# Moving a routing step, the last token transfer and the last weight casts in an attention and top-1 expert kernel

## The chip, the cores and the metric

The kernel runs on one core of one Trainium2 chip. The metric is the device time of one execution in microseconds (us). Before the change three runs took 266.01, 266.17 and 263.75 us, with a median of 266.01. One more execution was profiled.

## The reference

Linear attention without softmax over 8 batches of 8 heads, 576 tokens and 64 columns a head; its output, normed and laid out as 4608 tokens of 512 columns, goes through a layer of 8 experts, of which each token uses the one with the highest gate logit.

```python
kv = np.einsum('bhsd,bhse->bhde', k, v)
out = np.einsum('bhsd,bhde->bhse', q, kv)
rms = np.sqrt(np.mean(out * out, axis=-1, keepdims=True) + 1e-06)
x = out / rms * g_norm                 # as (4608, 512)
logits = x @ w_gate
expert_idx = np.argmax(logits, axis=1)
# gate_w: softmax probability of the chosen expert
h = np.maximum(x[expert_idx == e] @ w1[e], 0.0)      # 512 -> 1024
out[expert_idx == e] = gate_w * (h @ w2[e])          # 1024 -> 512
```

All inputs are drawn at random in f32.

## The kernel before, in words

The order of the instructions on every engine is written by hand (`manual_schedule`): an engine runs its instructions in the order in which the program emits them, and a waiting instruction holds up those behind it. There are three stages.

**Attention, in slots.** Before the loop, 92 products of zeros (`zeros`, L876, 64 columns each) run on PE while the first k and v load. Then 36 slots of 128 tokens follow. In slot `s`, `x_mm(s)` (L343) multiplies 128 transposed q rows by the batch's kv matrix, which holds the gate's columns as well; `x_qt(s+2)` (L320) transposes a later q block; `x_norm(s)` squares the product (`sq`, ACT, L361) and sums it (`ms`, DVE, L365). From slot 31 on the rest of a slot, `held`, comes one slot late: logarithm and exponential on ACT (`lnt`, `rinv`), the scaled logits (`lr`, DVE, L373) and the scaled rows (`xh`, DVE, L381). What else a slot does is put on lists by `at(list, slot, function)`: `mid` runs straight after `x_mm`, `pre` after `sq` and `ms` are issued, `late` near the end of the slot.

**Routing, in groups of 2 to 5 slots.** For each group, class `Route` finds the expert of each token and the token's row within that expert's part of the scratch tensor `xs_scratch`: `logits`, `top`, `below` (`dl`), `code`, `first`, `choose`, `tally` (`cum`, L445) on DVE; `expo` (ACT, L469, `ex`, the exponentials for the gate); `ranks`, three products on PE (L461, L462, L465) that write into unused columns of the PSUM tile of a slot; then `mask` (L473), `send` (row numbers `sli`, L481, and gate sums, L483) and `total` (L453) on DVE; and `scatter`, one indirect DMA for each slot, issued by POOL (L491). The list `plan` gives each group's slots in the order sum, below, one-hot, rank, then the slots of its scatters. Group (3, 0, 4), the first four slots of the last pair of batches, is the one whose entry changes. The next group, (3, 4, 3), is the `rt` of the lines after `plan`; the last one is called `end`.

**Experts.** `jobs[e]` holds expert e's tokens: 608 for each of the first seven, 672 for the last, which is given an expert with many tokens. `fetch` reads them on SP's queue: the marks `mt` (L683, and L691 for the last 32 tokens of job 7) and a transposing DMA `xt` (L675). `one` multiplies by w1 (L731) and applies relu on ACT (L743); `two` multiplies by w2 (L797), 128 tokens a tile; `put` scales on DVE (`ys`, L805) and POOL scatters the rows to the output (L808). Job 7 has a sixth tile of 32 tokens, spread over 128 partitions (L789). For expert 0, the first 384 tokens are fetched when the routing of most slots is done (`jobs[0].fetch(0, NE)`, in slot 30), so that its first products (`early_one`, `early_pair`, tile `hpe`) run between the last routing steps. The rest of its tokens (tile `hpl`) waits for all scatters.

Weights arrive on SP's queue in f32 (`load1` at L165 and `load2` at L171, 2 MB each) and are cast to f16: w1 on DVE (L177) or ACT (L183), w2 on ACT (L188, `cast2`) or, where `cast2` is given an engine, on DVE (L190). SP's queue is one line: loads and fetches are issued and moved in the program's order. In the loop over experts, iteration n runs job n and issues, after its `one` products, the next load and then the fetch of job n+3. In iteration 4 that load is w2 of expert 7, and the fetch behind it is job 7's. During iteration n the weights of expert n+1 are cast: w1 in the first half of the `one` products, w2 between the tiles of `two`.

Of the kernel before, what the change touches and what calls it, by code (L numbers as in the profile page):

```python
# [21 lines left out]
def _bc(ap: bass.AP, insert_pos: int, count: int) -> bass.AP:  # L22
    dims = [list(d) for d in ap.ap]
    dims.insert(insert_pos, [0, count])
    return bass.AP(tensor=ap.tensor, offset=ap.offset, ap=dims)
# [3 lines left out]
def kernel(  # L29
# [11 lines left out]
    nc = tc.nc  # L41
# [4 lines left out]
    E = 8  # L46
    F = 1024
    RW = 516
    CT = 5
# [3 lines left out]
    NE = EARLY // 128  # L53
# [142 lines left out]
    def load_next(count=1):  # L196
        nonlocal n_loads
        for _ in range(count):
            if n_loads < len(loads):
                n, m = loads[n_loads]  # L200
                (W[n].load1 if m == 1 else W[n].load2)(stg[n_loads % 5], nc.sync)
                n_loads += 1
# [93 lines left out]
    def split(s):  # L296
        P, r = divmod(s, 9)
        b = 2 * P + (r >= 4)
        return P, r, b
# [34 lines left out]
    def x_mm(s):  # L334
        P, r, b = split(s)
        if r < 8:
            parts = [(slice(0, 128), kvs_bufs[b % 4])]
        else:
            parts = [(HALF[tok], kvs_bufs[(2 * P + tok) % 4]) for tok in range(2)]
        ops[s] = quad("kvp" if s in (32, 35) else "op", "op")  # L340
        for i4 in range(4):
            for cols, kvs in parts:
                nc.tensor.matmul(  # L343
                    ops[s][cols, i4, 0:144], qts[s][:, i4, cols], kvs[:, i4, :],
                    start=True, stop=True,
                )

    def x_norm(s):
        P, r, b = split(s)
        if r == 0:  # L350
            xgs[P] = xh[P % 2][:, 0:9 * RW].rearrange("p (g c) -> p g c", g=9)
            lrs[P] = PW.tile([128, 9, 8, 8], F32, tag="lr", bufs=2, name="lr")
        if r == (2, 2, 2, 3)[P]:
            nc.gpsimd.tensor_copy(
                xgs[P][:, :, 512:514].bitcast(I32).rearrange("p g o -> p (g o)"),
                tokc[:, 9 * P:9 * P + 9],
            )
        xg, lr = xgs[P], lrs[P]
        oc = ops[s]
        sq = PW.tile([128, 8, 64], F32, tag="sq", bufs=1, name="sq")  # L360
        nc.scalar.activation(  # L361
            sq.rearrange("p (c i) n -> p c (i n)", i=2), oc[:, :, 0:128], ACTF.Square
        )
        ms = PW.tile([128, 8], F32, tag="ms", bufs=3, name="ms")
        nc.vector.reduce_sum(ms, sq, axis=AXX)  # L365

        def scale():
            lnt = PW.tile([128, 8], F32, tag="lnt", bufs=3, name="lnt")
            nc.scalar.activation(lnt, ms, ACTF.Ln, scale=1.0 / 64.0, bias=epsb)
            rinv = PW.tile([128, 8], F32, tag="rinv", bufs=3, name="rinv")  # L370
            nc.scalar.activation(rinv, lnt, ACTF.Exp, scale=-0.5)  # L371
            r2 = rinv.rearrange("p (c i) -> p c i", i=2)
            nc.vector.tensor_tensor(  # L373
                lr[:, r, :, :].rearrange("p (c i) n -> p c i n", i=2),
                oc[:, :, 128:144].rearrange("p c (i n) -> p c i n", i=2),
                _bc(r2, 3, 8), op=ALU.mult,
            )
            return r2

        def rows(r2):  # L380
            nc.vector.tensor_tensor(  # L381
                xg[:, r, 0:512].rearrange("p (i c n) -> p c i n", i=2, c=4),
                oc[:, :, 0:128].rearrange("p c (i n) -> p c i n", i=2),
                _bc(r2, 3, 64), op=ALU.mult,
            )

        def rest():
            r2 = scale()
            return lambda: rows(r2)

        return rest
# [441 lines left out]
    def expert_at(t):  # L833
        return nc.values_load(
            tabi[0:1, 0, bass.ds(t, 1)], engines=[ENG.SP],
            min_val=0, max_val=E - 1,
        )
# [16 lines left out]
    jobs = []  # L854
# [10 lines left out]
    with tc.tile_pool(name="psattn", bufs=1, space=bass.MemoryType.PSUM) as PSA:  # L865
        first_slot = [9 * (b // 2) + 4 * (b % 2) for b in range(B)]
        mid, pre, head, late, last = ({s: [] for s in range(-4, 40)} for _ in range(5))

        def zeros(count, tag="misc", bufs=1, n=512):
            warm = PSA.tile([128, 4, 256], F32, tag=tag, bufs=bufs, name="warm") \  # L870
                if tag == "op" else PSA.tile([128, 2, 256], F32, tag=tag, bufs=bufs, name="warm")
            warm = warm[:, 0:2, :].rearrange("p a c -> p (a c)")

            def more(count, n=512):
                for _ in range(count):
                    nc.tensor.matmul(  # L876
                        warm[:, 0:n], blank[:, 0:64].bitcast(F16),
                        blank[:, 0:n // 2].bitcast(F16), start=True, stop=True,
                    )
            more(count, n)  # L880
            return more

        def at(where, s, fn, *args):
            where[s].append(lambda: fn(*args))

        for b in range(1, B):
            f = first_slot[b]
# [23 lines left out]
            ((1, 5, 4), (18, 19, 20, 21), (22, 23, 24, 25)),  # L911
            ((2, 0, 5), (23, 24, 25, 26), (26, 27, 28, 28, 29)),
            ((2, 5, 4), (27, 28, 28, 29), (29, 29, 30, 30)),
            ((3, 0, 4), (31, 31, 31, 32), (32, 33, 33, 34)),
        ]
        for g, (s_sum, s_below, s_oh, s_rank), s_scat in plan:
            rt, G = Route(*g), g[2]
            at(late, s_sum, rt.logits, 0, G)
            at(late, s_below - (s_below == s_oh > s_sum), rt.top)
            at(late, s_below, rt.below)  # L920
            at(late, s_below, rt.code)
            at(late, s_oh, rt.expo)
            at(late, s_oh, rt.first)
            at(late, s_oh, rt.choose)
            at(late, s_oh, rt.tally)
            at(late if s_rank == 32 else mid, s_rank, rt.ranks, s_rank)
            at(late, s_rank, rt.mask)
            at(late, s_rank, rt.send)
            at(late, s_rank + (g[0] < 2), rt.total)
            for t, slot in enumerate(s_scat):  # L930
                at(late, slot, rt.scatter, t, t + 1)
        at(last, 2, load_all, ("k", 4), ("v", 4))
# [18 lines left out]
        rt = Route(3, 4, 3)  # L951
        at(late, 34, rt.logits, 0, 3)
        at(late, 34, rt.top)
        at(late, 34, rt.below)
        at(late, 34, rt.expo)
        at(late, 34, rt.code)
        at(late, 34, rt.first)
        at(late, 34, rt.choose)
# [45 lines left out]
                    g2[half, :], None, op0=ALU.mult,  # L1004
                )

        more = zeros(92, "op", 2, 64)
        for m, piece in enumerate(KV_PIECES):
            kv_mm(0, *piece)
            if m == 1:  # L1010
# [62 lines left out]
        job = jobs[0]  # L1073
        job.hidden()
        x_mm(35)
        rest = x_norm(35)
        relu = [job.early_one(0, "qtp"), job.early_one(1, "misc")]
        rt.ranks(34)
        rt.mask()
# [62 lines left out]
    if True:  # L1142
        for n in range(E):
            job = jobs[n]
            nxt = jobs[n + 1] if n + 1 < E else None
            if n > 0:
                job.hidden()
            spans = job.spans if n > 0 else []
            if n == 1:
                spans = [(AHEAD, CAP)]  # L1150
            for ws, (c0, c1) in enumerate(spans):
                for f in range(8):
                    job.one(f, c0, c1)
                    if n > 0 and ws == 0 and f % 2 == 1 and nxt is not None:
                        W[n + 1].cast1(f // 2)
            if nxt is not None:
                load_next()
            if n + 3 < E:
                jobs[n + 3].fetch()
            for t in range(NE if n == 0 else 0, job.nt):  # L1160
                job.two(t)
                if n > 0 and t < 4 and nxt is not None:
                    W[n + 1].cast2(t)
            if n == 0:
                rest_of_table = left_over_table()
                for e in range(FIXED, E):
                    ev = expert_at(e)
                    W[e].e = jobs[e].row = bass.ds(ev, 1)
            if nxt is not None:
                nxt.place(NA if n == 0 else 0)  # L1170
                load_next()
            if n == 2:
                rest_of_table()
            if n in (2, 5):
                nc.gpsimd.drain()

    nov = nc.values_load(tabi[0:1, 1, 7:8], min_val=0, max_val=NOV)
    with tc.If(nov > 0):
        with tc.For_i(0, nov) as t:
            w = Weights(bass.ds(expert_at(t + 8), 1), 0)  # L1180
            job = left_over(t, w, 0, 0, out_views[E * CT + 1])
# [40 lines left out]
```

## Time and profile before

| what | before |
|---|---|
| median of three runs | 266.01 us (263.75 to 266.17) |
| profiled execution, its own time | 265.15 us |
| span of the profile, first to last instruction | 263.3 us |
| PE busy, share of the span | 241.4 us, 92% |
| weight loads on PE (PEld) | 173.9 us, 66% |
| ACT busy | 158.9 us, 60% |
| DVE busy | 139.0 us, 53% |
| POOL busy | 101.5 us, 39% |
| DMA | 83.13 MB, 316 GB/s over the span |
| SP's queue (q1), share of 16 DMA engines | 78.2% |
| mean granted clock of PE | 0.986 |

The profile is of one execution. PE, DVE, ACT and POOL are engines, SP issues transfers; a name with q, as SPq, is an engine's sequencer. A row of the timeline gives start, duration, engine, line, operation and the tile written and read; in square brackets stands how long the engine was idle just before, and what ended that. The attention and its routing take the first 124 us, the experts the rest.

### The profile page before, as it was taken

What the parts mean: (1) busy time and instruction counts of PE and PEld (TensorE: products, weight loads), DVE (VectorE), ACT (ScalarE), POOL (GpSimd) and SP (SyncE); (2) the same over time, 40 slices, a digit from 0 to 9 for tenths busy, and PEclk for the clock granted to TensorE, in tenths of its full rate; (3) what the DMA queues carried; (4) which work ended last, traced back from release to release, by engine and by line L of the source; (5) the groups of instructions that cost most, each with busy time, mean ns of one, the idle gap of its engine ahead of it and who ended that gap; (6) DMA issues with size and microseconds to landing.
All of it is one profiled execution on the core that took longest, in us unless ns stands there. A gap on an engine that the chain in (4) does not pass through costs nothing.

```text
span 263.3 us, 7015 instructions
## 1 busy us (share of the span) xinstructions
PE 241.4 (92%) x2786; PEld 173.9 (66%) x2786; DVE 139.0 (53%) x374; ACT 158.9 (60%) x356; POOL 101.5 (39%) x131
## 2 busy tenths in 40 slices
PE   7779888989999998688989999999999999998991
PEld 7679877878879887564666466574664756645640
DVE  0105576768788686778607761497344163351041
ACT  1146757577676789579494658286465738736600
POOL 4032222676377377356602240512405215042044
PEclk9979999999999999799999999999999999999999
DMA  7999999999999999599699997999999999995022
GB/s 226 386 391 391 391 410 375 393 396 390 389 394 401 412 410 400 235 192 356 176 259 258 406 406 121 316 410 242 358 410 253 389 308 321 421 241 186 1 108 100
DMA packets 52106, 83.13 MB, mean 316 GB/s; under 512 B 27862, under 2 KB 27990, under 8 KB 51944
## 3 DMA queue, kind: packets, MB, share of 16 engines
q1 hardware_dynamic: 46900, 68.28, 78.2%
q0 software_dynamic: 4848, 14.20, 14.3%
q10 hardware_dynamic: 324, 0.19, 0.6%
q8 instruction: 22, 0.36, 0.6%
q14 instruction: 12, 0.10, 0.1%
HBM read 63.42 MB, written 16.17 MB: 302 GB/s over the span
## 4 chain that ended last, share of the span: by engine, by line
PE 30%; issue 27%; DMA 13%; ACT 11%; POOL 10%; DVE 5%; POOLq 1%; SPq 0%; ACTq 0%
PE op L343 11%; POOL out_dram L808 10%; DMA out_dram<-ys,idx 9%; PE kvp L252 6%; PE qtp L320 5%; ACT sq L361 3%; DMA land<-in_q_dram 3%; DMA land<-in_v_dram 2%; PE ype L797 2%; ACT w1b L183 2%; DVE ms L365 2%; PE hpa L731 1%; PE yp L797 1%; ACT kvs L263 1%; ACT qts L326 1%
## 5 line engine op out<-in xcount | busy, mean ns | idle before, releaser
L808 POOL DMA_INDIRECT out_dram<-ys,idx x41 | 40.3, 983 | 94.5 <-DVE ys L805 87.9
L797 PE MATMUL yp<-w2b,xh 128*128 128x512 f16 (+1 forms) x296 | 65.2, 379 | 0.6 <-ACT xh L778 0.6
L731 PEld LDWEIGHTS <-w1b 128*128 128x128 f16 x512 | 49.9, 98 | 21.6 <-issue 3.1
L743 ACT ACTIVATE xh<-hp 128x304 f16<-128x304 f32 (+2 forms) x104 | 44.8, 431 | 28.6 <-PE hp L731 17.0
L731 PE MATMUL hp<-xt,w1b 128*128 128x304 f16 (+2 forms) x416 | 56.4, 296 | 1.3 <-DMA xt<-xs_scratch 1.3
L797 PEld LDWEIGHTS <-xh 128*128 128x128 f16 (+1 forms) x320 | 32.6, 102 | 35.8 <-issue 0.8
L805 DVE TENSOR_SCALAR ys<-yp,gate 128x512 f32<-128x512 f32 (+2 forms) x38 | 27.9, 739 | 51.1 <-PE yp L797 51.1
L343 PE MATMUL op<-kvs,qts 128*128 128x144 f32 (+1 forms) x320 | 46.1, 304 | 0.6 <-ACT kvs L291 0.6
L491 POOL DMA_INDIRECT xs_scratch<-xh,sli x36 | 35.5, 985 | 23.9 <-issue 9.7
L343 PEld LDWEIGHTS op<-kvs,qts 128*128 128x128 f32 (+1 forms) x320 | 39.3, 187 | 3.7 <-ACT kvs L291 0.8
L188 ACT CAST w2b<-land 128x1024 f16<-128x1024 f32 x30 | 29.3, 1042 | 14.3 <-DMA land<-in_moe_w_dram 14.3
L365 DVE TENSOR_REDUCE ms<-sq 128x8 f32<-128x512 f32 x36 | 24.7, 685 | 22.1 <-ACT sq L361 21.3
L310 POOL COPY qp<-land 128x512 f32<-128x512 f32 x32 | 19.4, 613 | 36.1 <-DMA land<-in_q_dram 24.6
L361 ACT ACTIVATE sq<-op 128x512 f32<-128x512 f32 x36 | 21.4, 595 | 16.1 <-PE op L343 12.0
L177 DVE TENSOR_SCALAR w1b<-land,g 128x1024 f16<-128x1024 f32 x26 | 18.0, 749 | 15.1 <-DMA land<-in_moe_w_dram 15.1
L252 PE MATMUL kvp<-land 64*64 64x64 f32 x1152 | 24.1, 223 | 1.9 <-DMA land<-in_v_dram 1.0
L320 PE MATMUL qtp<-ident,qp 128*128 128x128 f32 x144 | 23.2, 284 | 2.5 <-POOL qp L310 1.1
L381 DVE TENSOR_TENSOR xh<-op,rinv 128x512 f16<-128x512 f32 x36 | 24.5, 681 | 0.3 <-PE op L465 0.3
L252 PEld LDWEIGHTS kvp<-land 64*64 64x64 f32 x1152 | 20.0, 134 | 6.6 <-issue 5.8
L326 ACT COPY qts<-qtp 128x512 f32<-128x512 f32 x36 | 21.0, 583 | 4.7 <-PE qtp L320 4.6
L320 PEld LDWEIGHTS qtp<-ident,qp 128*128 128x128 f32 x144 | 17.4, 146 | 3.4 <-issue 1.8
L373 DVE TENSOR_TENSOR lr<-op,rinv 128x64 f32<-128x64 f32 x36 | 8.0, 222 | 12.0 <-ACT rinv L371 8.6
(134 smaller groups left out, 170.2 us busy)
## 6 DMA issues: line engine op xcount, KB each, us to landing
land<-in_moe_w_dram SPq DMA_DIRECT2D x16, 2048.0 KB, 15.5
land<-in_q_dram SPq DMA_DIRECT2D x8, 1152.0 KB, 15.0
land<-in_k_dram SPq DMA_DIRECT2D x7, 1152.0 KB, 16.6
land<-in_v_dram SPq DMA_DIRECT2D x7, 1152.0 KB, 17.8
land<-in_k_dram SPq DMA_DIRECT2D x2, 576.0 KB, 5.9
land<-in_v_dram SPq DMA_DIRECT2D x2, 576.0 KB
xs_scratch<-c_zero SPq DMA_DIRECT2D x1, 774.0 KB
out_dram<-ys,idx POOLq DMA_INDIRECT x41, 6.6
```

The costliest lines, as they stand in the source:

```text
L188: nc.scalar.copy(self.w2[:, part, :], self.s2[:, part, :])
L252: nc.tensor.matmul(kvst[b][HALF[ipar], hh, Dh * ip:Dh * ip + Dh], kb[HALF[hh], i, cols], vb[HALF[hh], i, cols], start=(j == 0), stop=(j == 8),
L320: nc.tensor.transpose(qtps[s][:, ip, :, tok, :], qps[s][:, tok, 2 * ip:2 * ip + 2, :], ident)
L343: nc.tensor.matmul(ops[s][cols, i4, 0:144], qts[s][:, i4, cols], kvs[:, i4, :], start=True, stop=True,)
L361: nc.scalar.activation(sq.rearrange("p (c i) n -> p c (i n)", i=2), oc[:, :, 0:128], ACTF.Square)
L365: nc.vector.reduce_sum(ms, sq, axis=AXX)
L491: go = nc.gpsimd.indirect_dma_start(out=xs_views[9 * self.P + g0 + t], out_offset=IndirectOffsetOnAxis(ap=self.sli[:, t:t + 1], axis=0), i ...
L731: nc.tensor.matmul(hp, self.w.w1[:, 2 * (kk % 2) + kk // 2, f // 2 * 256:f // 2 * 256 + 256] .rearrange("p (m r) -> p r m", r=2)[:, f % 2, :],
L743: nc.scalar.activation(self.ht[:, f, c0:c1], hp, ACTF.Relu)
L797: nc.tensor.matmul(yp[0:m, :], self.ht[:, f, t * 128:t * 128 + m], self.w.w2[:, f, :], start=(f == 0), stop=(f == 7),)
L805: nc.vector.tensor_scalar(ys[0:m, 0:d], yp[0:m, 0:d], self.gate[0:m, t:t + 1], None, op0=ALU.mult)
L808: nc.gpsimd.indirect_dma_start(out=view, out_offset=IndirectOffsetOnAxis(ap=self.idx[0:m, t:t + 1], axis=0), in_=ys[0:m, 0:d], in_offset=None,
```

## The change

There are six edits. The zeros ahead of batch 0 become 72 products of 82 columns. Group (3, 0, 4) has its `expo` one slot later (32), its `ranks` on list `mid` of slot 33, with the same PSUM tile (slot 32's) as before, its `mask`, `send` and `total` on list `pre` of slot 33, and all four scatters in `late` of slot 33. Group (3, 4, 3) has its `expo` after slot 35's `sq`. The w2 casts of expert 7 go from ACT in iteration 6 to DVE in the first half of iteration 7's `one` products. Job 7's fetch goes ahead of the load of expert 7's w2. Job 7's tile of 32 tokens is computed third instead of last, so that its tiles run 0, 1, 5, 2, 3, 4.

```diff
-            ((3, 0, 4), (31, 31, 31, 32), (32, 33, 33, 34)),
+            ((3, 0, 4), (31, 31, 31, 33), (33, 33, 33, 33)),
...
-            at(late, s_oh, rt.expo)
+            at(late, s_oh + (s_rank == 33), rt.expo)
...
-            at(late if s_rank == 32 else mid, s_rank, rt.ranks, s_rank)
-            at(late, s_rank, rt.mask)
-            at(late, s_rank, rt.send)
-            at(late, s_rank + (g[0] < 2), rt.total)
+            then = pre if s_rank == 33 else late
+            at(mid, s_rank, rt.ranks, min(s_rank, 32))
+            at(then, s_rank, rt.mask)
+            at(then, s_rank, rt.send)
+            at(then, s_rank + (g[0] < 2), rt.total)
...
-        at(late, 34, rt.expo)
...
-        more = zeros(92, "op", 2, 64)
+        more = zeros(72, "op", 2, 82)
...
         rest = x_norm(35)
+        rt.expo()
         relu = [job.early_one(0, "qtp"), job.early_one(1, "misc")]
...
+                    if ws == 0 and f % 2 == 1 and nxt is None:
+                        job.w.cast2(f // 2, nc.vector)
+            if n + 4 == E:
+                jobs[n + 3].fetch()
             if nxt is not None:
                 load_next()
-            if n + 3 < E:
+            if n + 4 < E:
                 jobs[n + 3].fetch()
-            for t in range(NE if n == 0 else 0, job.nt):
+            order = list(range(NE if n == 0 else 0, min(job.nt, CT)))
+            if job.nt > CT:
+                order.insert(CT - 3, CT)
+            for t in order:
                 job.two(t)
-                if n > 0 and t < 4 and nxt is not None:
+                if n > 0 and t < 4 and nxt is not None and n + 2 < E:
                     W[n + 1].cast2(t)
```

## The prediction, made before the changed kernel was run

> **What bounds the kernel now.** I read the waits of PE first, since PE is busy 92% of the span; this is the view for 100 us to the end (who waited for whom: us in total, times, longest).
>
> ```profile
> PE op L461 <- ACT sq L361: 2.0, 1, 2.0
> PE hp L731 <- DMA xt<-xs_scratch: 1.3, 1, 1.3
> ...
> PE hpl L731 <- DMA xt<-xs_scratch: 0.4, 1, 0.4
> PE hpe L731 <- DMA xt<-xs_scratch: 0.4, 1, 0.4
> ```
>
> Only two waits are long: 2.0 us at `ranks` (L461) and 1.3 us for a token transfer. The timeline shows what the first is made of and what stands behind it.
>
> ```profile
> 107.64 0.23 ACT L469 ACTIVATE ex<-dl 128x32 f32<-128x32 f32 x1 [1.37 <-DVE dl L418]
> 107.78 0.71 ACT L183 ACTIVATE w1b<-land,g 128x512 f16<-128x512 f32 x1
> ...
> 108.39 0.57 ACT L361 ACTIVATE sq<-op 128x512 f32<-128x512 f32 x1
> 108.46 0.22 DVE L445 TENSOR_TENSOR_SCAN cum<-ch,oh 128x32 f16<-128x32 f16 x1
> ...
> 109.01 0.19 PE L461 MATMUL op<-csum,ones 128*128 128x32 f16 x1 [1.97 <-ACT sq L361]
> ...
> 111.75 1.64 SPq L675 DMA_TRANSPOSE xt<-xs_scratch  x1
> ...
> 116.02 1.46 PE L731 MATMUL hpe<-xt,w1b 128*128 128x384 f16 x8 [0.35 <-DMA xt<-xs_scratch]
> ...
> 117.31 0.18 PE L461 MATMUL op<-csum,ones 128*128 128x24 f16 x1
> ...
> 118.55 0.17 DVE L473 TENSOR_TENSOR t<-op,oh 128x24 f32<-128x24 f32 x1
> ```
>
> ACT sat 1.37 us before `ex`, with slot 32's `sq` queued behind it, and `ranks` writes where `sq` reads, so PE stood still. But seven us later PE waits again, for expert 0's tokens, which land at 116.0. The third view is the table by stretches, cut at the 3.41 us steps of the granted clock (length, then busy us of PE, PEld, DVE, ACT, POOL; then the clock).
>
> ```profile
> 9.96:13.37 3.41, 2.58 (x79) 1.63 (x77) 0.96 (x7) 0.73 (x2) 0.00 (x0) 1.00 1.04 389
> 13.37:16.78 3.41, 2.12 (x27) 1.66 (x28) 0.00 (x0) 1.50 (x4) 2.27 (x4) 1.00 1.06 393
> 16.78:20.20 3.42, 3.42 (x17) 3.41 (x16) 0.40 (x1) 1.31 (x3) 0.00 (x0) 0.50 1.05 388
> ...
> 105.53:108.95 3.42, 1.35 (x10) 0.99 (x10) 2.67 (x9) 2.05 (x6) 2.04 (x4) 1.00 0.90 359
> 108.95:112.36 3.41, 3.35 (x16) 2.96 (x16) 1.87 (x7) 1.80 (x6) 0.76 (x1) 0.50 0.18 69
> ```
>
> A stretch with PE busy 2.12 of 3.41 us (62%) or 1.35 us (39%) is followed by one at half clock; one with 2.58 us (76%) isn't. Last, SP's queue and the end of the timeline:
>
> ```profile
> 133.27 9.04 SPq L675 DMA_TRANSPOSE xt<-xs_scratch  x1
> ...
> 217.97 0.37 SPq L171 DMA_DIRECT2D land<-in_moe_w_dram  x1
> ...
> 225.26 9.98 SPq L675 DMA_TRANSPOSE xt<-xs_scratch  x1
> ```
>
> ```profile
> 235.64 2.32 PE L797 MATMUL yp<-w2b,xh 128*128 128x512 f16 x10
> ...
> 239.26 9.28 PE L731 MATMUL hp<-xt,w1b 128*128 128x336 f16 x64 [1.30 <-DMA xt<-xs_scratch]
> ...
> 258.24 0.98 POOL L808 DMA_INDIRECT out_dram<-ys,idx  x1 [0.74 <-DVE ys L805]
> 259.53 0.98 POOL L808 DMA_INDIRECT out_dram<-ys,idx  x1 [0.30 <-issue]
> ```
>
> From 139.9 to 237.96 PE has no wait; the one wait after that is for job 7's `xt`, which stands in SP's queue behind 4 MB of weights.
>
> **The change part by part.** *Zeros.* 92 products took 5.09 us at about 53.3 ns, 64 columns at half clock. 72 of 82 columns make 5904 columns against 5888: the same 4.9 us, and behind them PE waits 1.0 us for v anyway. 0, either way under 0.1.
>
> *The routing step of group (3, 0, 4).* With `ex` a slot later, ACT runs slot 32's `sq` after the cast of slot 31 (0.71 us), at about 106.9 instead of 108.39. `ranks` no longer stands ahead of slot 33's `x_mm` on PE, which starts after `x_qt(34)` (end 107.05) and two zero products, about 107.5 instead of 109.90. `ranks` then comes at 108.7, when `cum` ends (108.46 + 0.22). Behind it on PE stand `x_qt(35)` and `x_mm(34)`; the latter must wait for slot 31's rows on DVE in any case (about 110.1), so the added wait costs nothing. On DVE the moved `mask`, `send` and `total` (0.6 us, 110.33 to 110.90 before) now stand ahead of slot 32's `lr` and `xh`; POOL gets the rows about 0.5 us later (sli about 111.2 for 110.73), and its four scatters, 1.27 us apart, end before the next group needs POOL. Following DVE, the engine with least slack here, row by row with the durations above (`ms` 0.6, `lr` and `xh` 0.8, routing of a group 1.85), slot 35's `x_mm` ends near 113.2 instead of 115.66, 2.5 us earlier.
>
> *Where that goes.* The tokens of expert 0 don't come earlier. SP's transfer at 111.75 waits for scatters of earlier groups, the last issued by POOL at 106.18, and lands at 115.97. PE's next instructions are the eight `hpe` products that read it, and the last-but-one `ranks` stands behind those, at 117.31 before and after. Only DVE's queue ahead of `mask` at 118.55 gets shorter: at full clock it would run at 117.55, 1.0 us earlier, and the rest of the routing, the scatters, the second fetch and the experts behind it with it. But PE is now idle from 113.2 to 116.0, 2.8 us. By the rows above, 1.3 us of idle time in a step of 3.41 us halved the next step. Wherever the steps lie, a gap of 2.8 us puts 1.3 us into one of them (3.41 + 2.8 - 2 x 1.3 = 3.6, more than a step). So one step of half clock begins between 114.5 and 117.9 and falls on the `hpe` products: eight take 2.6 us instead of 1.3. Worked through for starts across that interval, the third block of `hpe` (121.83) comes 0 to 0.4 us later than before. The Trainium skill ("TensorE: Matmul & The Clock Gate", Why this matters for your kernels) warns only of idle gaps over about 3 us; by that rule the clock stays up and the step gives -1.0. This trace halved the clock after gaps of less than 2 us, so the row decides: +0.2, with -1.0 and +0.4 as the ends.
>
> *`expo` of group (3, 4, 3)* goes behind slot 35's `sq` on ACT (0.22 us); its result is needed at `send` over a us later. 0; without that cover 0.2.
>
> *Job 7's fetch ahead of w2.* PE's job 6 ends at 237.96, and at other changes of job the next product starts 0.17 us before that modelled end (204.00 against 204.17): 237.79 instead of 239.26, -1.47. For that `xt` must land 1.5 us earlier. It goes past a 2 MB load that takes about 5 us at some 400 GB/s (383 to 393 in the last column above), so it lands near 234. What is late next is w2. SP can issue it only when it is done with the transposing transfer: 9.04 us at 133.27, where likewise one load stood ahead, so from 219.5 to about 229; 10.1 us from there to landing (the shortest of L171) with job 6's output beside it give 239 to 241. The four casts on DVE (L190, 0.69 us each) end by 244. w2 is needed when job 7's `two` starts, 248.2 - 1.47 = 246.8. Cover: nearly 3 us.
>
> *Casts from ACT to DVE.* ACT loses 4 x 1.04 us in job 6, where nothing waits for it; DVE gains 2.8 us where it was idle for 11 us. A rule of the Trainium skill speaks against it: "SBUF — State Buffer", Who interferes with whom, says that a cast on DVE in a two-port mode shuts GpSimd out, descriptor writing too. The row: POOL's scatter at 123.26, beside two L190 casts, took 1.23 us against 0.96 for its neighbours. By the row 0.3, by the rule up to 0.7 on a scatter of job 6; POOL's next work is 10 us later, so 0 by both.
>
> *The 32-row tile third.* Its 32 products take about 0.63 us of PE wherever they are. Last on PE is now a full tile, at 257.19 + 0.63; DVE 0.75 and the usual 0.27 put its scatter at 258.86 instead of 259.53. But it needs longer: 2.73 us from issue to landing (258.24 to 260.97) against 2.16. -0.1; with the 3.84 us of the slowest tile of this job +1.0.
>
> **The sum**: +0.2 - 1.47 - 0.1 = -1.4 us. The profiled execution, 265.15 (span 263.3, and 1.85 around it), becomes 263.8. The median of three is 266.01, but the runs are spread over 2.4 us and the profiled one lies inside; the median of all four is 265.58, from which -1.4 gives 264.2, my prediction, 0.7% under 266.01.
>
> **The rivals.** *The clock stays up* over the 2.8 us gap, or PE isn't idle so long: both gains arrive, -1.0 - 1.47 - 0.1 = -2.6, 263.0. For it: the waits at 109.01 and 118.55 are real. Against it: the two halved steps. *The transfer is hidden anyway*: job 7's `xt` is early, but job 6 or `xt` of jobs 5 and 6, which land only some 1.3 us ahead of PE, hold PE up instead: about 0, 265.6. Against it: the edit touches nothing ahead of the load of w1 of expert 7. *Slower: w2 comes too late.* If SP stays 15.9 us in the transposing transfer, as at 144.51 and 165.36, w2 is issued at 235.4, and with the median 15.5 us lands at 250.9; job 7's `two` would begin at 251.6 instead of 246.8, +4.8, or 3.4 in all: 269. It decides from a landing at 246.1, and passes the old time from 247.5. Against it: those transfers had two loads ahead, this one has one.
>
> **How the numbers follow.** Likeliest case 0.57, own range 263.0 to 265.6 (half the 2.4 us spread of the runs to either side; its unknown costs, +0.2 and +1.1 at most, lie within); clock stays up 0.24; hidden anyway 0.12; w2 late 0.07. A measurement of this kernel can tell about 1% (2.7 us) from no change: below 263.3 counts as faster. That holds most of the second case and a fifth of the first: 0.28. Slower, above 268.7: 0.07. Between: 0.65. The range 262.0 to 266.6 leaves out the late w2 and the edges of the others.
>
> **What would show it.** Right: PE's 1.97 us at L461 gone and slot 33's `x_mm` near 107.5; a wait of more than 2 us for `xt` ahead of the first `hpe`, with half clock in the next step; job 7's first product with no wait; w2's DVE casts done before 245; the last scatter 0.5 to 0.8 us earlier against job 7's `two`. Wrong: full clock through 114 to 121, a wait of PE at L797 for a cast, or w2's landing after 246.

## The result, and the profile after

The changed kernel took 266.51 us (median of 22 runs, 263.63 to 268.05), the kernel before, run beside it, 265.88 us (22 runs, 263.75 to 267.01). The ratio is 1.0013, with a 95% interval from 0.9991 to 1.0036: no difference that can be measured, where 264.2 us and 0.7% less had been forecast. The profiled execution of the changed kernel took 263.98 us (span 262.0), 1.2 us less than the profiled one of before; it is not a typical one, for 15 of the 22 runs had a mean clock of 0.980 or less and 265.6 us or more, and the profiled one has 0.985. Ratios here leave out single runs more than 1.5% above the fastest of their kernel.

In the profiled pair the forecast's sum nearly came true (-1.2 us for -1.4), and so the lines that answer to those of before mislead as to the whole. The terms of the expert stage came true there; the routing step took another path than forecast. First PE's waits from 100 us to the end (who waited for whom: us in total, times, longest).

```profile
PE hpl L731 <- DMA xt<-xs_scratch: 1.7, 1, 1.7
...
PE hpe L731 <- DMA xt<-xs_scratch: 0.7, 1, 0.7
```

The wait of 2.0 us at L461 and the one of 1.3 us ahead of job 7 are gone. A wait of 0.4 us at `hpl` has become one of 1.7. The timeline around the moved routing step:

```profile
108.50 0.59 ACT L361 ACTIVATE sq<-op 128x512 f32<-128x512 f32 x1
...
109.89 0.23 ACT L469 ACTIVATE ex<-dl 128x32 f32<-128x32 f32 x1
110.01 0.18 PE L461 MATMUL op<-csum,ones 128*128 128x32 f16 x1
...
113.75 1.20 PE L343 MATMUL op<-kvs,qts 128*64 128x144 f32 x16 [0.31 <-ACT sq L361]
...
115.68 1.46 PE L731 MATMUL hpe<-xt,w1b 128*128 128x384 f16 x8 [0.73 <-DMA xt<-xs_scratch]
...
117.49 0.17 DVE L473 TENSOR_TENSOR t<-op,oh 128x24 f32<-128x24 f32 x1
```

`ex` now stands behind `sq`, and the products of L461 wait for nobody. But `x_mm` of slots 18 to 32 starts 1.7 to 1.9 us later than before, for a reason further ahead in the program: `x_mm(33)` starts at 109.03 (109.90 before, 107.5 forecast), `x_mm(35)` at 113.75, only 0.7 us earlier than before (114.46), and PE is at the first `hpe` product just 0.7 us ahead of the tokens. The clock stays full from 114 to 121 us, which the forecast had named as a sign of being wrong. The next `mask` runs at 117.49 for 118.55. Last, SP's queue, PE, the casts and the last scatter:

```profile
219.50 9.56 SPq L675 DMA_TRANSPOSE xt<-xs_scratch  x1
...
229.30 0.40 SPq L171 DMA_DIRECT2D land<-in_moe_w_dram  x1
...
238.03 9.28 PE L731 MATMUL hp<-xt,w1b 128*128 128x336 f16 x64
...
239.48 2.45 DVE L190 CAST w2b<-land 128x1024 f16<-128x1024 f32 x4
...
247.15 3.62 PE L797 MATMUL yp<-w2b,xh 128*128 128x512 f16 x16
...
257.68 0.98 POOL L808 DMA_INDIRECT out_dram<-ys,idx  x1 [0.74 <-DVEq L1186]
```

Job 7 starts without a wait, 16.90 us after job 6 (at 221.13) instead of 18.36 after it. w2 is issued at 229.30, and its casts are done by 241.93, 5.2 us ahead of job 7's `two`. The last scatter comes 10.53 us after that `two` began, not 11.15.

The clock is the view in which the changed kernel looks worse, at the start (length of the stretch, then busy us of PE, PEld, DVE, ACT, POOL; then the granted clock, the DMA share and GB/s).

```profile
11.89:15.30 3.41, 1.60 (x17) 0.83 (x17) 0.00 (x0) 1.32 (x3) 0.75 (x2) 1.00 1.05 397
15.30:18.72 3.42, 3.42 (x27) 3.06 (x28) 0.00 (x0) 1.34 (x4) 1.58 (x3) 0.50 1.05 389
18.72:22.13 3.41, 3.41 (x17) 3.40 (x16) 0.69 (x1) 1.73 (x5) 0.00 (x0) 0.50 1.06 393
```

Two steps at half clock follow each other from 15.30, where before had one (16.78 to 20.20). One step lowers the mean clock of a run by 0.5 x 3.41 / 263 = 0.0065, and costs up to 1.7 us where PE sets the time.

### The profile page after: what moved, and what is told of

It is laid out like the page before. It is cut to its first block, busy times and chain, and to the rows that moved or that the text cites. A ratio compares the mean times of both kernels' runs of the same rounds, so it can differ in the third digit from the quotient of the medians.

```text
span 262.0 us, 6975 instructions
## 1 busy us (share of the span) xinstructions
PE 240.5 (92%) x2766; PEld 173.1 (66%) x2766; DVE 141.4 (54%) x378; ACT 155.2 (59%) x352; POOL 101.4 (39%) x131
## 5 line engine op out<-in xcount | busy, mean ns | idle before, releaser
L343 PEld LDWEIGHTS op<-kvs,qts 128*128 128x128 f32 (+1 forms) x320 | 38.7, 185 | 6.3 <-ACT rinv L371 2.0
L188 ACT CAST w2b<-land 128x1024 f16<-128x1024 f32 x26 | 25.4, 1042 | 6.2 <-DMA land<-in_moe_w_dram 6.2
L369 ACT ACTIVATE lnt<-ms,epsb 128x8 f32<-128x8 f32 x36 | 10.8, 301 | 5.7 <-DVE ms L365 5.6
```

What stands on the lines that cost most here:

```text
L188: nc.scalar.copy(self.w2[:, part, :], self.s2[:, part, :])
L343: nc.tensor.matmul(ops[s][cols, i4, 0:144], qts[s][:, i4, cols], kvs[:, i4, :], start=True, stop=True,)
```

## The experiments

There are eighteen runs of fifteen kernels, in turns of two or four on one chip each, five chips in all. The kernel before was run in the same turns each time; the ratio is to it, and the interval behind it is the 95% one. Of each run the profile of one execution is at hand, and the time and mean clock of 11 or 12.

**Which part?** My theory A: the expert stage gains, and the routing edit gives it back in half-clock steps. Theory B: the expert stage gains, and the zeros, which I had put at nothing, take it back by the clock. Theory C: the gain of the expert stage itself is lost in most runs.

e1 is the kernel before with the three edits of the expert stage alone:

```diff
+                    if ws == 0 and f % 2 == 1 and nxt is None:
+                        job.w.cast2(f // 2, nc.vector)
+            if n + 4 == E:
+                jobs[n + 3].fetch()
...
+                order.insert(CT - 3, CT)
...
```

> The three edits of the expert stage alone (job 7's fetch ahead of w2, its w2 casts on DVE, its 32-row tile third). Theory A (the expert stage gains what its wait was worth, and the routing edit gives it back through half-clock steps): -1.3 to -1.6 us against the kernel before in every run, at unchanged clock; job 7's first product with no wait. Theory B (the zeros cost the clock at the start): the same here, -1.3 to -1.6. Theory C (the gain of the expert stage is lost in most runs, since a transfer holds job 7 up in another way): -0.5 to +0.5, and a wait for xt or for a cast of w2 in job 7.

Measured: 263.77 us against 265.01, ratio 0.9938 (0.9900 to 0.9977), mean clock 0.988 (before 0.985). The forecast of 1.3 to 1.6 us lies within the 0.6 to 2.7 us of this interval; C falls.

e2 is the routing edit alone, the new entry of `plan` and the two moves of `expo`:

```diff
-            ((3, 0, 4), (31, 31, 31, 32), (32, 33, 33, 34)),
+            ((3, 0, 4), (31, 31, 31, 33), (33, 33, 33, 33)),
...
```

> The routing edits alone (ranks, mask, send and total of group (3, 0, 4), and both moved exponents). Theory A: +0.5 to +2 us in the median, more half-clock time in the slower runs, PE waiting for expert 0's tokens over 1 us ahead of the first hpe product. Theory B: -0.3 to +0.3. Theory C: -0.3 to +0.3, its gain on PE lost again at the wait of hpl for the second fetch.

Measured: 265.46, ratio 1.0006 (0.9973 to 1.0039), clock 0.986: no gain and no loss that can be measured.

e3 is the zeros alone:

```diff
-        more = zeros(92, "op", 2, 64)
+        more = zeros(72, "op", 2, 82)
```

> The zeros alone: 72 products of 82 columns. Theory A: within 0.3 us of the kernel before. Theory B: +1 to +2 us in the median, half-clock time of two steps instead of one after 13 us. Theory C: within 0.3 us.

Measured: median 265.78, 0.8 us over before, ratio 0.9997 (0.9951 to 1.0043, from 7 of the 12 runs), mean clock 0.978; 9 of 12 runs at 0.980 or less. The clock speaks for B, the time does not decide.

e4 is the whole change with the old zeros:

```diff
-        more = zeros(72, "op", 2, 82)
+        more = zeros(92, "op", 2, 64)
```

> The whole change, but with the 92 zero products of 64 columns. Theory A: like the whole change, within 0.5 us of the kernel before. Theory B: -1.3 to -1.6 us against the kernel before. Theory C: like the whole change.

Measured: 263.69, ratio 0.9963 (0.9933 to 0.9993), clock 0.987. With the old zeros the change gains; A falls as the main cause.

**Is it the zeros, on one chip?** The pair that carries the verdict was run last, side by side: the whole change (n1) and the same with the old zeros (n2, the diff of e4).

> The whole change, beside the same with the old zeros on one chip. Theory B (in the whole change the 72 zeros of 82 columns cost the gain through the clock, wherever the half-clock steps then fall): mean clock 0.978 to 0.982, ratio 0.997 to 1.002, and 1 us or more slower than the other kernel of this call. Rival H (the zeros make no difference; what was seen so far was chance or chip): both kernels within 0.5 us of each other, ratios 0.994 to 0.998.

> The whole change with the old 92 zeros of 64 columns. Theory B: mean clock 0.985 or more, ratio 0.993 to 0.997, 1 us or more faster than the other kernel of this call. Rival H: within 0.5 us of it.

Measured: n1 266.26, ratio 1.0008 (0.9970 to 1.0045), mean clock 0.977; n2 264.67, ratio 0.9965 (0.9935 to 0.9995), clock 0.983; before 265.52. The medians are 1.6 us apart, the ratios 0.0043 (1.1 us), and the mean clock differs by the worth of one half-clock step: B holds, H does not. The whole change was measured in three turns (1.0013, 0.9974 as g1 below, 1.0008) and with the old zeros in two (0.9963, 0.9965); weighted by their intervals these give 1.0003 and 0.9964, so that the zeros cost about 1.0 us (0.3 to 1.7). Over all runs of the whole change, the mean clock is 0.979 with 72 of 82 (46 runs of three turns) and 0.985 with 92 of 64 (24 runs), 0.985 in 162 runs of before.

**What about the zeros?** Two properties changed at once: they are wider, and they end earlier (5.78 us for 6.27 in the profiled pair). g1 is the whole change again; g2 has `zeros(88, "op", 2, 82)`, wide and long, g3 `zeros(82, "op", 2, 64)`, narrow and short. Theory B1: the early end costs; B2: the width costs; rival D: g1 gains after all.

> The whole change once more, beside the variants below on one chip. Theory B (72 zeros of 82 columns lower the clock at the start; the other parts gain 1.0 to 1.7 us): no gain against before (ratio 0.998 to 1.004), most runs at a mean clock of 0.972 to 0.980, the profiled one with two half-clock steps in a row near 15 to 22 us or a later first full step. Rival D (the change gained nothing on its first chip for another reason, and gains where the old zeros gained): 0.994 to 0.997 here too, clocks of 0.985 and above.

> The whole change with 88 zeros of 82 columns: as wide, but longer, so that they end at about 6.1 to 6.5 us instead of 5.8 and PE is idle 1.0 us or less ahead of v. Theory B1 (what costs is that the zeros end early, so that PE is idle 1.9 us instead of 1.0): the clock recovers, most runs above 0.980, ratio 0.993 to 0.997, as with the old zeros. Theory B2 (what costs is the width of 82, or that zeros of this shape raise the clock a step earlier, and its evaluation falls on the thin stretch around 12 to 15 us): as the whole change, ratio 0.998 to 1.004, clocks of 0.972 to 0.980 in most runs.

> The whole change with 82 zeros of 64 columns: as narrow as before, but ending about as early as 72 of 82 (82 x 55.3 ns = 4.5 us). Theory B1 (the early end costs): as the whole change, ratio 0.998 to 1.004, clocks of 0.972 to 0.980 in most runs. Theory B2 (the width costs): the clock stays up, ratio 0.993 to 0.997.

Measured, with 265.28 for before: g1 265.63, 0.9974 (0.9938 to 1.0010), clock 0.981; g2 265.09, 0.9975 (0.9949 to 1.0000), clock 0.982; g3 264.00, 0.9941 (0.9915 to 0.9967), clock 0.984. The interval of g1 leaves D open; n1 above, run later on another chip, speaks against it. g3 and g1, which differ in the zeros alone, are 1.6 us apart in the medians, but their intervals overlap. The order speaks against B1; g2 in the middle says little.

k3 (88 of 82) and k4 (82 of 64) put the same two shapes into the kernel before.

> The kernel before with 88 zeros of 82 columns alone: as wide as the change's, but as long as the old ones. Mean clock over its runs against that of the kernel before (0.985 so far; with 72 of 82 it was 0.978 to 0.981 in 46 runs of three kernels). If the width costs: 0.982 or less and 0.5 us or more slower. If the early end costs: 0.984 to 0.987 and the time of before within 0.5 us.

> The kernel before with 82 zeros of 64 columns alone: as narrow as the old ones, but ending at 5.8 us like the change's. If the early end costs: mean clock 0.982 or less and 0.5 us or more slower than before. If the width costs: 0.984 to 0.987 and the time of before within 0.5 us.

Measured, with 265.53 for before: k3 265.47, 0.9979 (0.9949 to 1.0009), clock 0.988; k4 264.21, 0.9994 (0.9961 to 1.0027), clock 0.980. The clock says B1 here, against g3, and the median of k4 is lower than that of k3 in spite of it. Neither B1 nor B2 explains all four.

**Where does the routing gain go?** g4 has the old zeros, and the 2 MB load of w1 of expert 2 behind the second fetches:

```diff
-        at(last, 32, load_next, 1)
...
         jobs[1].fetch(NA, CT)
+        load_next(1)
```

> The whole change with the old zeros, and the 2 MB load of w1 of expert 2 issued behind the second fetches of experts 0 and 1 instead of behind slot 32 (about 132 us instead of 115.5). Theory E (the routing edit's gain of 1.0 us is lost because the last scatters land behind this load: issue at 122.8, landing at 127.8 with the load, about 2.6 us after issue without it): the second fetch is issued at about 125.5, PE's wait of 2.5 us at hpl is gone or under 0.5, no half-clock step near 133, and yp comes 2 to 3.5 us earlier than 138.2: ratio 0.984 to 0.990. Rival F (the second fetch is held by something else, or the load is late for later jobs): the wait at hpl stays above 1.5 us, ratio 0.994 to 1.000; or a new wait for weights of expert 2 or 3 appears in jobs 1 to 3 and eats the gain.

Measured: 266.99, ratio 1.0046 (1.0011 to 1.0081). Rival F's second half: with one load more to pass in jobs 1 to 6, PE waits 2.7 us in two places for the tokens of a job. Theory E wasn't tested by it: after a wait of 3.6 us at `hpe` and a half-clock step the last scatter was issued at 125.74, not at 122.8.

k1 puts zero products into that wait (on the whole change with the old zeros); k2 has them too, and the load between the two second fetches. The fill in both:

```diff
...
+        zeros(12)
         relu = [job.early_one(0, "qtp"), job.early_one(1, "misc")]
...
```

> The whole change with the old 92 zeros of 64 columns, and 12 zero products of 512 columns (2.6 us) on PE between x_mm(35) and the first hpe product, where PE waits 3 to 4.4 us for the tokens of expert 0. Theory of the prediction's third step (the gap halves the clock under hpe, and that alone costs the routing edit its gain of 1.0 us): no half-clock step between 114 and 123, the last scatter is issued at about 122.8 and yp comes about 1 us or more earlier than without the fill in the profiles with the half step: ratio 0.989 to 0.992. Theory E (the gain is lost a second time at the second fetch, whose scatters land at about 127.6 whenever they are issued): no half step at hpe, but PE waits 2 us or more at hpl and the step after it is at half clock; ratio 0.993 to 0.998, as without the fill.

> As k1, and the 2 MB load of w1 of expert 2 issued between the second fetches of expert 0 and expert 1. Theory E: the scatters land 2.6 us after issue (about 125.5), hpl starts near 130.3 without a wait over 0.5 us, yp near 134.5 instead of 136.2 to 138.2: ratio 0.980 to 0.987 if job 1's tokens (now behind the load in SP's queue) still land by 138. Rival G (the load's new place moves the hold-up on): PE waits 1 us or more for the tokens of job 1 or 2, ratio 0.990 to 1.002.

Measured: k1 263.65 us, ratio 0.9924 (0.9900 to 0.9948), clock 0.988, and no run at 0.980 or less; k2 265.96, 1.0010 (0.9978 to 1.0041), clock 0.996. In k2 the new place of the load cost 1.9 us of waits for tokens: rival G. In k1 no half-clock step came at `hpe`, as the theory of the third step had it, and the ratio is just outside its 0.989 to 0.992; but the last scatter was issued at 124.92, not at 122.8, and m4 below, the same kernel on another chip, had only 0.9965. The view by stretches shows what the fill does:

```profile
114.31:117.72 3.41, 3.41 (x21) 1.57 (x17) 2.67 (x9) 1.66 (x7) 2.65 (x3) 1.00 1.07 216
117.72:121.14 3.42, 3.35 (x25) 1.93 (x23) 2.29 (x11) 2.15 (x6) 1.65 (x3) 1.00 0.92 310
```

PE is busy all through and the clock stays full, where n2, without the fill, has this:

```profile
112.71:116.12 3.41, 0.05 (x2) 0.08 (x1) 2.47 (x9) 1.68 (x6) 2.80 (x3) 1.00 1.18 231
116.12:119.53 3.41, 2.66 (x12) 1.30 (x12) 0.00 (x0) 0.49 (x1) 0.04 (x1) 0.50 0.95 242
119.53:122.95 3.42, 3.00 (x23) 1.73 (x22) 2.83 (x14) 2.39 (x5) 1.93 (x2) 1.00 1.03 419
```

**The four shapes behind the fill.** m1 to m4 are k1 with 72 of 82, 82 of 64, 88 of 82 and 92 of 64.

> The whole change (72 zeros of 82 columns) plus only the 12 zero products of 512 columns ahead of hpe, which took the lottery of the clock out of that place. What is left of it comes from the start. Theory B (these zeros cost the clock at the start): mean clock 0.978 to 0.983, half or more of the runs at 0.981 or less, 1 to 2 us slower than with 92 of 64 in this call: ratio 0.996 to 1.000. Rival H (the change's lost gain was at hpe alone, and the start costs nothing): mean clock 0.986 or more, ratio 0.991 to 0.994.

> The same with 82 zeros of 64 columns: they end as early as 72 of 82. If the early end costs (B1): mean clock 0.978 to 0.983, 1 to 2 us slower than 92 of 64. If the width costs (B2): 0.986 or more, as 92 of 64.

> The same with 88 zeros of 82 columns: as wide as the change's, as long as the old ones. B1: mean clock 0.986 or more and the time of 92 of 64. B2: 0.978 to 0.983 and 1 to 2 us slower.

> The whole change with the old 92 zeros of 64 columns and the fill, once more as the measure for the three others: ratio 0.990 to 0.995, mean clock 0.986 to 0.990, no run under 0.982.

Measured, on a chip where the kernel before took 268.51 us (265.49 to 274.33): m1 267.00, 0.9970 (0.9933 to 1.0008), clock 0.985; m2 266.72, 0.9941 (0.9901 to 0.9982), clock 0.987; m3 269.24, 1.0019 (0.9973 to 1.0064), clock 0.984; m4 267.73, 0.9965 (0.9925 to 1.0005), clock 0.988. The intervals overlap, and the order is neither by width nor by end: neither B1 nor B2 is borne out. With the gap at `hpe` filled, no cost of 72 of 82 against 92 of 64 is seen (0.9970 and 0.9965). That fits a cost that comes mostly through that gap, but each of the two is known to 0.4% only, as much as is looked for, so it does not show it.

## Why the prediction was wrong, point by point

**The zeros: "0, either way under 0.1". This is the step that failed.** In the whole change they cost about 1.0 us (0.3 to 1.7; by the medians of n1 and n2 1.6). With the old zeros the change gives 0.9963 and 0.9965, and the forecast of -1.4 us lies within both intervals. I counted the zeros' own length and the wait behind them, and not what they do to everything later. The rows show three such things; the runs show what the zeros cost in all, but not the share of each.

*Half steps at the start.* In four of the five profiles with 72 of 82 two half-clock steps in a row fall between 7 and 23 us, and one in the fifth; with 92 of 64 it is none or one in nine profiles (though two of those reach full clock only at 14 us). No time is lost by this up to the 129th product of `x_mm`: it begins at 60.4 us in the mean of the five profiles, and at 61.2 in that of the nine with 92 of 64.

*The place of the clock's steps.* All changes of the clock in one execution lie on one grid of 3.41 us. From the start of the span, modulo 3.41, the grid stands at 0.50 to 2.35 us in the eight profiles with zeros of 82 columns, and between 1.91 and 3.78 in the twelve with 64 (3.78 being 0.37 of the next period). So with the wide zeros the grid lies over a us earlier in the mean, and with it changes which gap is cut by which step. At `hpe` this shows: n1 (72 of 82) and g2 (88 of 82) have two half-clock steps in a row there, n2, g3 and g4 one. The rows of n1, to be held against those of n2 above:

```profile
113.14:116.56 3.42, 0.39 (x7) 0.22 (x4) 2.80 (x9) 1.66 (x7) 2.51 (x3) 1.00 0.95 204
116.56:119.97 3.41, 2.59 (x10) 1.21 (x10) 0.00 (x0) 0.66 (x2) 0.37 (x1) 0.50 1.13 254
119.97:123.39 3.42, 3.42 (x15) 1.66 (x14) 2.82 (x14) 2.26 (x4) 1.92 (x2) 0.50 0.96 345
```

In n2 the gap ends 0.75 us into the next step, PE is busy for 2.66 us of that, and the clock comes back; in n1 it ends 0.82 us into it, with 2.59 us busy, and the clock stays down for one step more, up to 1.7 us. Whether this small difference decides it is not shown: in after the step from 15.30 was busy throughout, and a second half step followed all the same. The two spans (264.40 and 263.22) are 1.2 us apart, and this is there when job 1 starts (142.47 for 141.28): 0.5 us at the first `hpe` product, since the tokens came later (117.38 for 116.87), the rest behind the second half step, after which the last scatter is issued at 127.38 for 125.95. With the fill no half step begins between 111 and 258 us in any of six profiles (in m3 one begins at 110.77, ahead of the fill), and m1 and m4 can't be told apart: that agrees with it.

*PE's instructions.* Twenty products fewer are 40 instructions fewer on PE. The same stretch of PE's timeline in n1 and then in n2:

```profile
67.06 0.69 PE L252 MATMUL kvp<-land 64*64 64x64 f32 x32
69.65 1.22 PE L343 MATMUL op<-kvs,qts 128*128 128x144 f32 x8 [1.89 <-DVE xh L381]
```

```profile
68.07 0.69 PE L252 MATMUL kvp<-land 64*64 64x64 f32 x32
68.70 1.25 PE L343 MATMUL op<-kvs,qts 128*128 128x144 f32 x8
```

In n1 PE stands 1.89 us ahead of `x_mm`, in n2 it does not wait. The wait is put down to `xh`, but the program's waits are the same in both, and n2 doesn't wait for it. What is there is a transfer on the queue for instructions; in the 0.5 us from 67.0 of n1:

```profile
q8 instruction: 1, 0.02, 13.4%
```

(One packet, 0.02 MB.) It begins at 67.2 us, and PE goes on 2.5 us later. Of the 75 waits of PE over 0.3 us between 8 and 112 us that the 20 profiles put down to "issue", 56 end 2.2 to 2.75 us after such a 16 KB transfer began, and of those over 0.7 us all but one. In the four profiles with 72 products and no fill (the one of after among them: 1.88 us at 69.18) such a wait comes at this place, in none of the 16 others. The number of products alone doesn't set it: m1 has the same 72 ahead of it, its transfer began at 66.55, and PE did not wait. The slots behind it are 1.7 to 1.9 us late in the profile of after. In a whole change that still has to wait 3 to 4 us for tokens at `hpe`, this lateness is taken out of that wait; in g1 it is itself followed by a half-clock step (70.62 to 74.03). No run moved the instructions alone, so this part is read from rows, not tested.

**Routing of group (3, 0, 4): +0.2, from -1.0 to +0.4.** The size held: e2 is +0.2 us (-0.7 to +1.0), and in the profiled pair job 1 starts 0.2 us later (140.12 for 139.89). But both got there by another path than forecast, and that is luck. The mechanism held in five of the nine profiles with the routing edit and no fill. Of these, n2 has `x_mm(33)` at 106.84 (107.5 predicted), `x_mm(35)` 2.9 us earlier (2.5 predicted), then a wait of 4.1 us, longer than the 2.8 predicted since the tokens landed at 116.87 and not at 115.97, and half clock in the next step. The wait exceeds 3 us in the five (g2, g3, g4, n1, n2), and in all five the next step is at half clock; in the four others (after, e2, e4, g1) it is 1.3 us or less, and the clock stays up. So the rule that I took from the rows of before, that 1.3 us of idle time in a step halves the next, does not hold. In e2 PE was idle for 1.29 us of the step at `hpe`:

```profile
112.88:116.29 3.41, 2.12 (x23) 1.47 (x19) 3.17 (x11) 1.79 (x6) 2.50 (x4) 1.00 1.08 197
116.29:119.70 3.41, 3.05 (x22) 1.74 (x20) 2.90 (x15) 2.95 (x7) 2.78 (x3) 1.00 1.08 267
```

Over the steps of the 20 profiles up to 258 us, all 10 full-clock steps in which PE was busy for 1.35 us or less are followed by half clock, 19 of the 84 with more than that and less than 2.4 us, and none with more. In after the 1.0 us that I had dismissed did arrive at `mask` (117.49). It was lost one transfer on: the last scatter was issued 1.0 us earlier (123.76 for 124.79) and landed later (127.58 for 127.36), the second fetch went out at 127.76 for 127.54, and PE waited 1.7 us at `hpl`. In e2 and e4 this wait is 2.4 and 2.5 us and halves the clock in its turn, as e4 shows:

```profile
129.57:132.98 3.41, 0.94 (x10) 0.64 (x8) 0.11 (x1) 2.82 (x4) 0.00 (x0) 1.00 1.16 225
132.98:136.39 3.41, 3.41 (x21) 2.78 (x19) 0.29 (x3) 1.09 (x2) 0.00 (x0) 0.50 0.89 249
```

Why those scatters land at 127 to 128 us whenever they were issued before 124 stays open; that the load of w1 of expert 2, whose last part landed between 126.0 and 127.4 in the five profiles with such an early issue (after, e2, e4, g1, k4), holds them is likely, but g4 and k2 didn't test it, since their last scatters were issued at 125.74 and 124.94. The rule of the Trainium skill ("TensorE: Matmul & The Clock Gate", Why this matters for your kernels: beware of idle gaps over about 3 us) fits at `hpe`, where n2 and the four others lose the clock after one gap of 3.2 to 4.4 us and shorter ones leave it up; it does not fit at `hpl`, where e4 loses it after 2.5 us. Neither it nor my reading of the row was a safe guide.

**Job 7's fetch: -1.47.** Right in the pair: 16.90 us from job 6 to job 7 in every one of the 15 profiles with the edit. Perhaps mis-sized as a mean: in the five profiles with the old order (before, e3, e2, k3, k4) PE is held up by 1.46, 0.18, 0, 1.23 and 0 us, 0.6 in the mean. I had taken the largest. Why it varies stays open: a slower attention doesn't explain it, since job 1 starts earliest of all in k4 (139.13) and there is no wait there. Against a smaller size stands e1, where the stage gave 1.6 us (0.6 to 2.7). w2 was issued at 229.30 (about 229) and cast by 241.93 (244).

**`expo` and casts: 0.** Nothing waits for them in after's view of PE. POOL's scatter at 239.26, beside the casts on DVE, took 0.98 us like its neighbours; it began 0.22 us before the first of them.

**The 32-row tile: -0.1.** In the 15 profiles with it, the last scatter comes 10.53 us after job 7's `two` began, in the five without it 11.15: -0.62. From that scatter's start to the end of the span it takes 4.37 to 4.39 for 3.81 or 3.82: +0.56. The sum is -0.06.

**The rivals.** "Hidden anyway" (265.6) is nearest to the measured time, but not by its mechanism: the fetch was not held up elsewhere. "The clock stays up" came about at `hpe` in after, whose gain on PE was then lost at `hpl`, and with the fill in k1. w2 was late in none of the 15 profiles with the edit.

## What to carry to other kernels

Work ahead of the first load is not free to change because it ends before the load does: with another shape the clock's steps lay elsewhere against the rest of the program, and the whole change lost its gain of about 1.0 us; run such an edit by itself beside the others. A gain that makes an engine arrive earlier at a transfer is worth nothing until the transfer comes earlier too, and may cost a half-clock step: leave the edit out (e1, 0.9938), or try filling the gap with zero products (0.9924 in k1 and 0.9965 in m4, the same kernel; 0.9963 and 0.9965 without the fill in e4 and n2, so that its worth is not settled). A wait of one profiled execution is one draw; look for it in the profiles of kernels that do not touch it before it enters a sum.

## What the runs showed of the hardware

Between the first full-clock step and the last 4 us of the span, all half-clock stretches in the 20 profiles are one or two steps of one grid of 3.41 us, and the grid lay elsewhere with zeros of 82 columns (0.50 to 2.35 us) than with 64 (1.91 to 3.78). PE's instructions come in 22 transfers of 16 KB, mostly 6 to 8 us apart in the attention. Of the 25 waits of PE over 0.7 us between 8 and 112 us for which the profile names no releaser, 24 end 2.2 to 2.75 us after such a transfer began, and they last up to 2.0 us (m3); which transfers have a wait behind them, and why, stays open.
